# From which half batch on the feed-forward's input is turned by transposing DMAs: the 4th in place of the 6th

## The chip, the cores and the metric

The kernel runs on one core of one Trainium2 chip. The metric is the device time of one execution in microseconds (us). The engines of the core are named as the profile names them: PE (TensorE, matmuls), PEld (its weight loads), DVE (VectorE), ACT (ScalarE), POOL (GpSimd) and SP (SyncE, which here only issues DMAs). The core has 16 DMA engines.

## What is computed

Attention over 8 batches with 8 heads of 64 columns and 576 rows, with a mask that lets each block of 64 rows see itself and the blocks before it; then a feed-forward layer whose mixing step is a Fourier transform.

```python
scores = where(mask, q @ k.T / 8, -1e9)
attn   = softmax(scores) @ v                       # 64 heads of 576 x 64
x      = heads side by side                        # 8 batches, 576 x 512
u      = x + real(fft(fft(x, axis=1), axis=2))
un     = (u - mean(u)) / sqrt(var(u) + 1e-6)       # per row of 512
out    = u + relu(un @ w_ch1) @ w_ch2              # 512 -> 2048 -> 512
```

## The kernel before

All large matmuls run on halves of 16 bits: a number is split into a high part and a low part, and three products (high by high, high by low, low by high) replace one product of 32 bits.

**Stages.** For each head there are score matmuls (lines `scores`, out of the tiles `rest` and `lead`), a maximum over the scores (`max_part`, which reads `lead` alone), and value matmuls (`values`, into `av`). The rows of maxima are turned on PE (`shift`), shrunk on ACT to the small tile `mt` and copied by a DMA into one row of the head's `lead` tile, because the maximum is subtracted by the score matmul itself. Each batch of 8 heads then goes through the Fourier steps, and out of a batch come two half batches of 256 rows each (a lower and an upper one); the 64 rows that are left of each batch are gathered over four batches into one further half batch (the tiles `left`). So there are 18 half batches, numbered from 1: two for each of 8 batches, and the 9th and the 18th from the rows that are left. Each goes through normalization and through one feed-forward pass of matmuls (`first` into the tiles `h` and `ps`, `second` into `acc`).

**Heads and their tiles.** Heads are counted from 0. A head uses one of three pairs `lead0/rest0`, `lead1/rest1`, `lead2/rest2` in turn, so head 24 uses `lead0` and head 42 too. Queries and keys of two heads arrive together; their high and low parts are spread over the tiles by DMAs on SP's queue, `high_copies` (into `lead`, two DMAs of 64 x 576) and `low_copies` (into `rest`, two of 64 x 1152). The maximum of a head needs its high copies, its scores need the low copies and the `mt` copy as well.

**Turning.** The first feed-forward matmul needs the normalized rows `un` with the 512 columns on the partitions. There are two ways, and `BY_DMA` says from which half batch on the second is used:

```python
if me >= BY_DMA:      # norm, halve (ACT cast, DVE subtract), two transposing DMAs per 128 rows
    ...
    for n in range(2):
        sync.dma_start(parts[n][:, :, i], halves[:, n], transpose=True)
...
for c in range(NK):   # else four PE transposes of 128 x 128 per 128 rows, then ACT cast, DVE subtract
    tp(t[:, P * c:P * (c + 1)], un[:, P * c:P * (c + 1)], ident)
```

In the profile the PE transposes are the only instructions of L249; the copies of the second way are DMA_TRANSPOSE on SP's queue, `uh<-un` and `ul<-un`.

**The rows that are left.** For the second batch of each pair, after the last part of its Fourier step (matmuls of `zpc` and `zps`), four small DMAs gather 33, 31, 33 and 31 rows of 512 numbers into `left`:

```python
for at in (0, 64):
    sync.dma_start(mine[0][at:at + 33], X2[at:at + 33])
    sync.dma_start(mine[0][at + 33:at + 64], U2[at + 1:at + 32])
```

**Order.** The program is written by a planner at build time. Each piece of work is a `Step` with a cost on PE and a chain of costs on the other engines and on SP's queue (Q, M and L in a chain are the queue, the transfer and its latency); the planner keeps a clock of its own and issues the step that it takes to be ready, feed-forward matmuls as filler between the heads' work. Every engine runs its instructions in the order in which they were written, SP's queue too. A step that is added or taken away moves the planner's clock, and so the order of everything behind it. SP's DMAs carry one of eight counters in turn, so a DMA waits for the one eight places ahead of it.

Of the kernel before, what the change touches and what calls it, by code (L numbers as in the profile page):

```python
# [48 lines left out]
PSHIFT = 5  # L49


BY_DMA = 6
BANKS = {"ps": 3, "h": 2, "acc": 2}

ONCE = 17
# [164 lines left out]
def tile_attn_fourier_ffn(  # L220
# [857 lines left out]
    def normalized_steps(us, keys, stores, place):  # L1078
# [6 lines left out]
        def norm(i):  # L1085
# [11 lines left out]
            yield  # L1097
            if me >= BY_DMA and i == 0:
                yield from halve(i)

        def halve(i):
            un = uns.pop(i)
            halves = rows[i] = work.tile([P, 2, DM], F16, name="un", bufs=2)
            scalar.copy(halves[:, 0], un)
            yield
            vector.tensor_tensor(halves[:, 1], un, halves[:, 0], op=ALU.subtract)
            yield
# [27 lines left out]

        if me >= BY_DMA:
            free = (("F", me - 2),)
# [591 lines left out]
```

## Time and profile before

| | us |
|---|---|
| median of 3 timed runs (1200.2 to 1202.14) | 1201.1 |
| the profiled execution's own time | 1194.43 |
| its span, first to last instruction | 1192.6 |
| PE busy in it | 1116.1 (94%) |
| DVE, ACT, POOL busy | 744.6, 629.0, 479.6 |

The profiled execution is 6.7 us shorter than the median of the timed runs. Its span is read in three parts. Up to about 310 us PE is busy for 248.5 us and waits often; from 310 to 900 us heads and feed-forward passes run side by side and PE is nearly always busy; from 900 us on PE does feed-forward passes alone. The mean granted clock of PE is 0.987 of full speed. SP's queue holds 26 pairs of transposing DMAs, two for each of the half batches 6 to 18, the first at 454.3 us; the 40 PE transposes of half batches 1 to 5 end at 418.6 us.

### The profile page before, as it was taken

Reading aid. Unit: us, or ns where it says so; the run is one execution under the profiler, and the core shown is the slowest. Engines: PE = TensorE matmul, PEld = TensorE weight load, DVE = VectorE, ACT = ScalarE, POOL = GpSimd, SP = SyncE. Lnnn points to the kernel's source line nnn. Section 1 sums busy time; section 2 is a strip of 40 time slices with the busy share of each in tenths; the row PEclk is TensorE's granted clock in tenths of the full one; section 3 lists DMA queues with packets and bytes.
Section 4 is the critical chain, followed back from the end, with each engine's and each line's share of the span. In section 5 each row is a group of like instructions: output and inputs, shape, how many; then the busy total and the mean of one; then the engine's idle time right before and its main releaser. Section 6 shows DMA issues by size and latency. Waiting matters only on the chain.

```text
span 1192.6 us, 26123 instructions
## 1 busy us (share of the span) xinstructions
PE 1116.1 (94%) x10182; PEld 820.3 (69%) x10182; DVE 744.6 (62%) x1607; ACT 629.0 (53%) x1383; POOL 479.6 (40%) x621
## 2 busy tenths in 40 slices
PE   5766788999899999999999999999999999999998
PEld 4543465676677777777677777677766766888875
DVE  6886787677867767756476576666656434454421
ACT  5666768756775667656457557655223212334320
POOL 4452525444653535345224335443334210555410
PEclk9998989999899999999999999999999999999999
DMA  8776254343453238233335532460121021111100
GB/s 263 234 232 216 89 145 101 100 112 99 109 150 95 68 92 195 78 90 97 100 97 134 120 99 80 100 149 18 32 45 50 27 56 30 33 31 28 27 19 18
DMA packets 94049, 115.07 MB, mean 96 GB/s; under 512 B 37591, under 2 KB 64129, under 8 KB 93926
## 3 DMA queue, kind: packets, MB, share of 16 engines
q1 hardware_dynamic: 86582, 89.06, 28.2%
q10 hardware_dynamic: 4384, 16.78, 4.2%
q0 software_dynamic: 2960, 7.58, 2.3%
q8 instruction: 80, 1.31, 0.5%
q14 instruction: 43, 0.35, 0.1%
HBM read 58.50 MB, written 18.89 MB: 65 GB/s over the span
## 4 chain that ended last, share of the span: by engine, by line
PE 80%; DMA 5%; DVE 5%; POOL 3%; ACT 3%; issue 2%; SPq 0%; DVEq 0%; ACTq 0%; POOLq 0%
PE acc L246 28%; PE ps L246 26%; PE h L246 19%; PE av L246 7%; DMA lead<-mt 3%; POOL pl L213 2%; DVE W L213 1%; DMA lead<-rest 1%; POOL u L213 1%; DVE M L213 1%; ACT p L213 1%; ACT ph L213 1%; POOL ag L213 1%; DMA fs<-add 0%; SPq L213 0%
## 5 line engine op out<-in xcount | busy, mean ns | idle before, releaser
L213 POOL TENSOR_TENSOR pl<-p,ph 128x288 f16<-128x288 f32 (+1 forms) x256 | 262.8, 1037 | 352.3 <-ACT ph L213 183.1
L246 PEld LDWEIGHTS <-W 128*128 128x128 f16 x3456 | 331.0, 98 | 66.2 <-DVE M L213 6.3
L246 PE MATMUL acc<-W,gh 128*128 128x512 f16 (+1 forms) x1008 | 288.8, 369 | 0.0
L246 PE MATMUL ps<-uh,W 128*128 128x256 f16 x1184 | 217.0, 273 | 1.0 <-DVE M L213 1.0
L246 PE MATMUL h<-uh,W 128*128 128x256 f16 x1120 | 211.5, 275 | 4.9 <-DVE M L213 4.9
L246 PE MATMUL acc<-W,gl 128*128 128x512 f16 (+1 forms) x504 | 185.8, 369 | 1.0 <-DVE gl L213 1.0
L246 PE MATMUL ps<-ul,W 128*128 128x256 f16 x592 | 161.3, 272 | 0.0
L246 PE MATMUL h<-ul,W 128*128 128x256 f16 x560 | 153.7, 274 | 0.0
L246 PEld LDWEIGHTS <-ph 128*128 128x128 f16 x2112 | 132.2, 103 | 27.1 <-issue 3.9
L246 PEld LDWEIGHTS <-gh 128*128 128x128 f16 x1056 | 98.9, 99 | 69.5 <-issue 1.7
L213 DVE TENSOR_REDUCE M<-ps 128x1 fp32r<-128x320 f32 (+4 forms) x219 | 97.6, 480 | 66.4 <-PE ps L246 65.9
L246 PE MATMUL ps<-lead 73*128 73x288 f16 (+11 forms) x513 | 117.3, 293 | 13.6 <-ACT lead L213 6.2
L246 PE MATMUL av<-VH,pl 128*128 128x65 f16 (+1 forms) x963 | 116.7, 201 | 9.1 <-POOL pl L213 7.5
L246 PE MATMUL av<-VH,ph 128*128 128x65 f16 (+1 forms) x966 | 118.0, 203 | 1.9 <-ACT p L213 0.7
L246 PE MATMUL av<-VL,ph 128*128 128x64 f16 x960 | 116.3, 200 | 0.0
L246 PEld LDWEIGHTS <-pl 128*128 128x128 f16 x1056 | 103.1, 102 | 12.8 <-POOL pl L213 9.9
L213 ACT ACTIVATE p<-ps 128x288 f32<-128x288 f32 (+1 forms) x166 | 82.5, 498 | 46.3 <-PE ps L246 38.5
L213 ACT CAST ph<-p 128x512 f16<-128x512 f32 (+1 forms) x188 | 98.3, 523 | 4.9
L213 ACT ACTIVATE gh<-ps 128x512 f16<-128x512 f32 x74 | 44.0, 594 | 107.4 <-PE ps L246 105.9
L213 DVE SCALAR_TENSOR_TENSOR gl<-ps,gh 128x512 f16<-128x512 f32 x74 | 50.9, 688 | 79.4 <-ACT gh L213 78.7
L246 PEld LDWEIGHTS <-lead 73*128 73x128 f16 (+1 forms) x744 | 65.1, 103 | 40.5 <-issue 9.2
L246 PEld LDWEIGHTS <-gl 128*128 128x128 f16 x528 | 51.4, 97 | 57.1 <-DVE gl L213 2.7
(285 smaller groups left out, 1938.7 us busy)
## 6 DMA issues: line engine op xcount, KB each, us to landing
raw<-in_qk_dram SPq DMA_DIRECT2D x30, 576.0 KB
W<-in_moe_w_ch_dram ACTq DMA_DIRECT2D x14, 1024.0 KB
V<-in_v_dram SPq DMA_DIRECT2D x32, 320.0 KB
rest<-lead SPq DMA_DIRECT2D x64, 144.0 KB
rest<-rest SPq DMA_DIRECT2D x60, 144.0 KB
out_dram<-u SPq DMA_DIRECT2D x32, 256.0 KB
xd<-x SPq DMA_DIRECT2D x30, 256.0 KB
lead<-lead SPq DMA_DIRECT2D x60, 72.0 KB
```

Source lines behind the costliest of these rows:

```text
L213: x = f(*args, **kw)
L246: return tc.keep_in_program_order(nc.tensor.matmul(*args, **kw))
```

## The change

One number: half batches 4 and 5 (the upper half of the second batch, the lower half of the third) are turned by DMA too.

```diff
-BY_DMA = 6
+BY_DMA = 4
```

For these two half batches it takes away 16 PE transposes of 128 x 128, the 4 ACT casts and the 4 DVE subtractions that read their result out of PSUM; it adds 4 ACT casts and 4 DVE subtractions on `un` itself and 8 transposing DMAs on SP's queue. The program is the same up to the normalization of the 4th half batch, and the planner writes everything behind it in another order. Three places of that order follow.

**PE, at the 4th half batch.** The names: `lead_288` is `lead0` with head 24's high copies, `ps_4529` and `h_4559` take the transposes, `ph`, `pl` and `av` are values of head 22, `M_99` the maxima of head 23. Before, the two groups of transposes stand ahead of value matmuls, and head 24's maximum comes after 30 of these:

```order
L246 MATMUL ps_4455<-uh,W 128x256
L249 MATMUL ps_4529<-ident,un 128x128 x4
L246 MATMUL ps_4540<-ident,M_99 5x128
L246 LDWEIGHTS gh
L246 MATMUL acc<-W,gh 128x512
L246 LDWEIGHTS gh
L246 MATMUL acc<-W,gh 128x512
L246 LDWEIGHTS gl
L246 MATMUL acc<-W,gl 128x512
L249 MATMUL h_4559<-ident,un 128x128 x4
L246 LDWEIGHTS ph_4473
L246 MATMUL av<-VH_107,ph_4473 128x65
```

Now:

```order
L246 MATMUL h_4455<-ul,W 128x256
L246 LDWEIGHTS W
L246 MATMUL h_4455<-uh,W 128x256
L246 LDWEIGHTS lead_288
L246 MATMUL ps_4534<-lead_288 128x64
L246 LDWEIGHTS lead_288
L246 MATMUL ps_4534<-lead_288 128x64
L246 LDWEIGHTS lead_288
L246 MATMUL ps_4534<-lead_288 128x192
L246 LDWEIGHTS ph_4450
L246 MATMUL av<-VH_107,ph_4450 128x65
```

Behind the same 24 feed-forward matmuls, the same score matmuls of head 22 and the same turned maxima, head 24's maximum is now next: the 8 transposes are gone, and 3 matmuls into `acc` and 30 into `av` that stood ahead of it stand behind it.

**SP's queue at the same place.** `X_120` and `U_121` are the Fourier rows that are left; `lead_288<-lead_288` and `lead_288<-rest_289` are head 24's high copies. Before:

```order
L213 DMA left<-X_120 33x512 [waits DMAHW7_49,Pool_49]
L213 DMA left<-U_121 31x512 [waits DMAHW0_49,DMASW7_49,Pool_49]
L213 DMA left<-X_120 33x512 [waits DMAHW1_49]
L213 DMA left<-U_121 31x512 [waits DMAHW2_49,DMASW4_49]
L213 DMA lead_288<-lead_288 64x576 [waits DMAHW3_49,PE_49,Activation_49]
L213 DMA lead_288<-rest_289 64x576 [waits DMAHW4_49,Activation_49]
L213 DMA xd<-x 128x4x128 [waits DMAHW5_49,DVE_49]
L213 DMA xd<-x 64x128 [waits DMAHW6_49]
L213 DMA V<-in_v_dram 128x640 [waits DMAHW7_49,DVE_49]
L213 DMA lead_245<-mt 1x5x128 [waits DMAHW0_49,Activation_49]
L213 DMA rest_289<-rest_289 64x1152 [waits DMAHW1_49,DVE_49]
L213 DMA rest_289<-lead_288 64x1152 [waits DMAHW2_49,DVE_49]
```

Now, from the second of the copies on:

```order
L213 DMA lead_288<-rest_289 64x576 [waits DMAHW4_49,Activation_49]
L213 DMA xd<-x 128x4x128 [waits DMAHW5_49,DVE_49]
L213 DMA xd<-x 64x128 [waits DMAHW6_49]
L213 DMA lead_245<-mt 1x5x128 [waits DMAHW7_49,Activation_49]
L213 DMA V<-in_v_dram 128x640 [waits DMAHW0_49,DVE_49]
L213 DMA_TRANSPOSE uh<-un 128x4x128 [waits DMAHW1_49]
L213 DMA_TRANSPOSE ul<-un 128x4x128 [waits DMAHW2_49,DVE_49]
L213 DMA rest_289<-rest_289 64x1152 [waits DMAHW3_49,DVE_49]
```

Up to the second `xd<-x` the queue is unchanged, head 24's high copies behind the four copies of left rows included; the first pair of new transposes stands ahead of the low copies of heads 24 and 25 and of head 25's high copies.

**SP's queue at the next rows that are left** (fourth batch). Before, the `mt` copy of head 43 follows them after two `xd` copies:

```order
L213 DMA left<-U_121 31x512 [waits DMAHW1_49,DMASW6_49]
L213 DMA xd<-x 128x4x128 [waits DMAHW2_49,DVE_49]
L213 DMA xd<-x 64x128 [waits DMAHW3_49]
L213 DMA lead_535<-mt 1x5x128 [waits DMAHW4_49,Activation_49]
```

Now the `mt` copy of head 42 follows, with two low copies and a load of 576 KB between:

```order
L213 DMA left<-U_121 31x512 [waits DMAHW4_49,DMASW6_49]
L213 DMA xd<-ZT 2x256 [waits DMAHW5_49]
L213 DMA rest_536<-rest_536 64x1152 [waits DMAHW6_49]
L213 DMA rest_536<-lead_535 64x1152 [waits DMAHW7_49]
L213 DMA raw<-in_qk_dram 128x1152 [waits DMAHW0_49]
L213 DMA lead_288<-mt 1x5x128 [waits DMAHW1_49,Activation_49]
```

Another head's `mt` copy is the first behind the left rows, and more stands between.

## The prediction

> **What bounds the kernel now.** I read the page's shares first, then the stretches, then who makes PE wait.
>
> ```profile
> PE 1116.1 (94%) x10182; PEld 820.3 (69%) x10182; DVE 744.6 (62%) x1607; ACT 629.0 (53%) x1383; POOL 479.6 (40%) x621
> PE 80%; DMA 5%; DVE 5%; POOL 3%; ACT 3%; issue 2%; SPq 0%; DVEq 0%; ACTq 0%; POOLq 0%
> ```
>
> PE is 94% busy and 80% of the chain that ended last. The stretches of time say where the rest is:
>
> ```profile
> 0.00:310.00 310.00, 248.47 (x2169) 174.22 (x2170) 235.06 (x501) 207.86 (x471) 141.47 (x171) 0.95 0.53 157
> 310.00:600.00 290.00, 282.32 (x2932) 207.85 (x2929) 196.62 (x457) 180.03 (x401) 129.35 (x151) 1.00 0.41 107
> 600.00:900.00 300.00, 298.71 (x2842) 215.75 (x2841) 190.71 (x432) 159.46 (x348) 121.22 (x140) 1.00 0.34 87
> ```
>
> (Columns: length; busy time of PE, PEld, DVE, ACT, POOL; granted clock, DMA share, GB/s.) The program is unchanged up to the 4th half batch's normalization, near 317 us. Behind it PE is idle for 290 - 282.32 = 7.7 us up to 600 us and for 1.3 us up to 900 us. So there the end is set by PE work plus PE's few waits, and these waits are, from 310 us to the end:
>
> ```profile
> PE ps L246 <- DMA lead<-rest: 2.9, 2, 1.6
> PE h L246 <- DMA lead<-mt: 2.8, 1, 2.8
> PE h L246 <- DMA lead<-rest: 2.0, 1, 2.0
> PE ps L246 <- DVE M L213: 1.0, 1, 1.0
> PE acc L246 <- DVE gl L213: 1.0, 2, 0.7
> ```
>
> Most of the 9.7 us are waits for head copies. Whatever moves PE's arrival against such a copy moves the end.
>
> **The change part by part: the transposes.** The timeline of PE at the 5th half batch prices a group of four (the other group stands right ahead of it):
>
> ```profile
> 418.12 0.60 PE L249 MATMUL ps<-ident,un 128*128 128x128 f32 x4
> 418.56 0.27 PE L246 MATMUL ps<-uh,W 128*128 128x256 f16 x1
> ```
>
> From start to start a group costs 0.44 us, so the four groups that go are 1.76 us of PE. More is not there to gain from PE work. What replaces them, by tile `un`:
>
> ```profile
> L213 ACT CAST un<-un x26: 602/617/620, 421.7 to 1110.0; 128x512 f16<-128x512 f32 x26
> L213 DVE TENSOR_TENSOR un<-un x26: 680/691/1284, 422.4 to 1110.7; 128x512 f16<-128x512 f32 x26
> L213 SPq DMA_TRANSPOSE uh<-un x26: 1190/1225/2513, 454.3 to 1112.5; - x26
> ```
>
> Casts and subtractions read PSUM before and SBUF now, four of each both times; ACT and DVE are 62% and 68% busy from 310 to 600 us (180 and 197 of 290), so a few hundredths there are hidden behind PE: 0. The eight DMAs hold SP's queue for 8 x 1.22 = 9.8 us. What stands behind a pair comes up to 2.5 us later: the low copies of heads 24 and 25 and head 25's high copies at the first place, of which the nearest user, head 25's maximum, stands some 11 us of PE work behind head 24's in the new order. I put 0, and up to 2.5 us if the cover is gone.
>
> **The first place: the copies of head 24.** PE at the 4th half batch:
>
> ```profile
> 317.19 0.27 PE L246 MATMUL ps<-uh,W 128*128 128x256 f16 x1
> 322.62 0.39 PE L246 MATMUL acc<-W,gl 128*128 128x512 f16 x1 [0.31 <-DVE gl L213]
> 322.84 0.60 PE L249 MATMUL h<-ident,un 128*128 128x128 f32 x4
> 323.28 0.19 PE L246 MATMUL av<-VH,ph 128*128 128x65 f16 x1
> 324.15 0.19 PE L246 MATMUL av<-VH,pl 128*128 128x65 f16 x1
> 326.36 0.30 PE L246 MATMUL h<-lead 72*128 72x64 f16 x3 [2.02 <-DMA lead<-rest]
> 326.82 0.60 PE L246 MATMUL acc<-W,gh 128*128 128x512 f16 x2
> 327.48 0.59 PE L246 MATMUL acc<-W,gh 128*128 128x512 f16 x2
> ```
>
> From 317.19 (where the orders part) to 324.34 PE works through the rows shown ahead, then it waits 2.02 us for head 24's high copies. In the new order the same stretch lacks 8 transposes (0.88 us), 3 matmuls into `acc` (327.48 - 326.82 = 0.66) and 30 into `av` (323.28 to 324.15, 0.9), and the 0.31 us wait for `gl` goes with the `acc` group. So PE stands before head 24's maximum at 324.34 - 0.88 - 0.66 - 0.9 - 0.31 = 321.6. When do the copies land? SP's queue:
>
> ```profile
> 317.50 0.64 SPq L213 DMA_DIRECT2D left<-U  x1
> 318.18 0.80 SPq L213 DMA_DIRECT2D left<-X  x1
> 319.08 0.63 SPq L213 DMA_DIRECT2D left<-U  x1
> 319.81 0.52 SPq L213 DMA_DIRECT2D lead<-lead  x1
> 320.42 0.55 SPq L213 DMA_DIRECT2D lead<-rest  x1
> ```
>
> They are issued back to back with the left rows, nothing on SP waits for data, and yet they land near 326.2, 5.8 us after their issue. The left rows are the reason I see. Where they run alone (late in the program) the DMA share is one engine's sixteenth:
>
> ```profile
> 1058.00:1059.00 1.00, 1.00 (x12) 0.90 (x10) 1.00 (x2) 0.00 (x0) 0.96 (x3) 1.00 0.07 27
> ```
>
> At 27 GB/s the two copies of 31 rows, 62 x 2 KB = 127 KB, take 4.7 us on that engine, from about 319 on, and the copies' shares on it stand behind. [...] SP's queue is unchanged up to these copies, so they land at the same time, and PE now waits from 321.6 to 326.36: 4.8 us in place of 2.33. When it goes on, it still has the 30 and the 3 matmuls to do: 0.9 + 0.66 = 1.6 us behind. The 0.88 us of transposes taken away here gained nothing, since they lay ahead of a wait that ends when the DMA does. Those of the 5th half batch (417.7 to 418.6 us) lie where PE never stands still, so their 0.88 us is gained:
>
> ```profile
> 400.00:450.00 50.00, 50.00 (x523) 35.62 (x522) 35.69 (x87) 32.63 (x75) 25.77 (x34) 1.00 0.36 94
> ```
>
> Net idle and work: 1.6 - 0.9 = +0.7 us. Bounds: copies that land before 321.6 make it -1.76 - 2.33 = -4.1; copies a microsecond later make it +1.7.
>
> **What a wait of 4.8 us does to the clock.** Stretches of 3.41 us ahead of the half-clock spans, and three that were followed by none:
>
> ```profile
> 107.09:110.50 3.41, 1.23 (x3) 0.47 (x3) 2.02 (x6) 3.35 (x9) 0.81 (x2) 1.00 0.59 125
> 110.50:120.75 10.25, 6.94 (x21) 4.63 (x21) 5.99 (x13) 4.15 (x10) 0.44 (x3) 0.50 0.48 163
> 294.83:298.24 3.41, 1.53 (x7) 0.51 (x7) 3.24 (x14) 1.40 (x3) 2.64 (x4) 1.00 0.61 213
> 298.24:308.48 10.24, 7.54 (x68) 5.17 (x67) 8.58 (x14) 8.66 (x21) 7.53 (x10) 0.50 0.30 70
> 189.01:192.42 3.41, 1.60 (x10) 0.82 (x10) 3.36 (x11) 3.41 (x7) 0.00 (x0) 1.00 0.00 0
> 322.13:325.54 3.41, 1.91 (x36) 1.53 (x35) 3.25 (x5) 3.41 (x10) 2.29 (x2) 1.00 0.72 216
> 564.48:567.89 3.41, 1.89 (x23) 1.04 (x21) 1.14 (x3) 2.61 (x5) 2.83 (x4) 1.00 0.20 60
> ```
>
> A stretch with PE busy for 1.23 or 1.53 of 3.41 us was followed by 10.24 us at half clock; one with 1.60, 1.91 or 1.89 was not. The spans begin on one grid (298.24 - 110.50 = 55 x 3.413), and 322.13 lies on it. A wait of 4.8 us leaves at most 1.0 us of work in one of two neighbouring stretches, wherever the grid lies. So the half clock comes, and of its 10.24 us some 9.4 us are PE work at half speed: +4.7 us. That PE makes this up later is unlikely, since hardly a wait follows (9.7 us in the whole list, 2.3 of them here). [...] The rows show the half clock after stretches that were not idle, so I take 4.7.
>
> **The second place: the next left rows.** SP and PE there:
>
> ```profile
> 561.56 0.62 SPq L213 DMA_DIRECT2D left<-U  x1
> 563.43 0.73 SPq L213 DMA_DIRECT2D lead<-mt  x1
> 569.13 0.28 PE L246 MATMUL h<-lead 73*128 73x288 f16 x1 [2.76 <-DMA lead<-mt]
> ```
>
> The same pattern holds an `mt` copy for over 5 us and costs 2.76 us. In the new order head 42 is hit; its `mt` copy has a load and two low copies more ahead of it (a sixteenth of 576 KB and 2 x 144 KB is 54 KB, at 27 GB/s an estimated 2 us on the slow engine), and PE does some 1.4 us more work between, counted in the order. I take +0.6 us; from -2.76 (PE comes later than the copy) to +2, and a further 4.7 us if the clock falls there too.
>
> **Sum.** -0.9 + 1.6 + 4.7 + 0.6 = +6.0 us on the profiled execution's own 1194.43 us (its span 1192.6 and 1.8 around it): 1200.4. The timed median is 1201.1, 6.7 us above that execution. Its 2.0 and 2.8 us waits would put too little work into a stretch for some positions of the grid, so I suppose that timed runs pay the half clock at these places part of the time, and carry over +4 of the 6: 1201.1 + 4 = **1205 us**.
>
> **The rivals.** (1) No change: the timed runs before already pay the half clock at the first place, or it does not come. Then -0.9 + 1.6 + 0.6 = +1.3: 1202.4. [...] For the first: the unexplained 6.7 us. Against both: 1.91 us of work in the stretch at 322 us and no half clock, and half clock behind stretches with 1.23 and 1.53 us of work. (2) Faster: head 24's copies no longer hang on the left rows. `V`, 320 KB, is issued one place later than before; if it is that load which delays them, they land earlier, each microsecond earlier is one gained, and below 324.8 us the change pays: at 321.6 it is -4.1 and no extra half clock, 1197.0. Against it: the two copies of 31 rows stand ahead of them either way. (3) Slower still: the second place also falls to half clock and a transposing pair ahead of an `mt` copy opens a wait of up to 2.5 us: 6.0 + 4.7 + 2.5 - 2 = +11, 1212. Half clock there is decided by whether the wait passes about 3 us. Against it: 26 pairs stand in SP's queue before, and the list of waits above is short.
>
> **How the numbers follow.** Forecast 0.48, rival 1 0.22, rival 2 (with any other lucky order) 0.15, rival 3 0.15. A measurement of this kernel tells a change from none at about 0.2%, 2.4 us. Slower by more: 0.48 + 0.15 = 0.63; within: 0.22; faster: 0.15. The range from 1197.5 to 1212 reaches from rival 2 to rival 3 and leaves out about 0.15; the forecast's own range is 1203.5 to 1208.
>
> **What would show it.** In the changed profile: 24 PE transposes in place of 40 and 30 transposing DMAs into each of `uh` and `ul`; a PE wait of some 4.8 us for `lead<-rest` at 321 to 327 us and a granted clock of 0.50 for 10 us behind it; a wait for `lead<-mt` of 3 us or more at the fourth batch's left rows. I am wrong if PE does not wait over 3 us at the first place, or if the clock stays at 1.00 behind it; and a gain of more than 4 us would mean that waits I have not counted went away in the new order.

## The result

The changed kernel takes 1206.99 us (median of 10 runs, 1205.43 to 1212.83) beside 1200.65 us of the kernel before on the same chip (10 runs, 1197.15 to 1206.38). The ratio is 1.0061, with a 95% interval of 1.0046 to 1.0077: 6.3 us slower. Timed a second time (the ninth experiment) the ratio was 1.0085 (1.0059 to 1.0111).

The profiled execution of the changed kernel took 1206.64 us, its span 1204.8. The page answers the two rows shown of before so:

```profile
PE 1118.8 (93%) x10166; PEld 820.3 (68%) x10166; DVE 744.3 (62%) x1607; ACT 627.9 (52%) x1383; POOL 473.7 (39%) x621
PE 79%; DMA 6%; DVE 6%; POOL 3%; ACT 3%; issue 2%; SPq 1%; DVEq 0%; ACTq 0%; POOLq 0%
```

PE has 16 instructions fewer (10166 for 10182), and they are not shorter in sum: 1118.8 us busy against 1116.1, since more of them ran at half clock (mean granted clock 0.967 against 0.987). By stretches (same columns as before):

```profile
310.00:600.00 290.00, 280.65 (x2839) 204.91 (x2837) 190.76 (x450) 176.17 (x392) 124.26 (x148) 0.99 0.43 109
600.00:900.00 300.00, 294.10 (x2857) 212.56 (x2856) 178.62 (x413) 157.19 (x349) 112.54 (x133) 0.99 0.34 87
```

PE now stands idle for 9.4 us in the first stretch (7.7 before) and for 5.9 in the second (1.3 before). The list of waits from 310 us on:

```profile
PE ps L246 <- DMA lead<-rest: 7.4, 3, 4.7
PE ps L246 <- DMA lead<-mt: 3.6, 1, 3.6
PE h L246 <- DMA lead<-mt: 3.2, 1, 3.2
PE acc L246 <- DVE gl L213: 0.7, 1, 0.7
PE h L246 <- DMA rest<-lead: 0.4, 1, 0.4
```

These are 15.3 us where the five rows before were 9.7, and four waits make 13.8 of them. **The first place** is the one forecast:

```profile
323.70 0.27 PE L246 MATMUL h<-uh,W 128*128 128x256 f16 x1
328.69 0.33 PE L246 MATMUL ps<-lead 72*128 72x64 f16 x3 [4.72 <-DMA lead<-rest]
```

**The second** (3.2 us, at 577.8 us) is head 42's `mt` copy behind the fourth batch's left rows. **The third** (3.6 us, at 668.5 us) was not on my list. ACT writes head 49's `mt` rows:

```profile
663.41 0.27 ACT L213 ACTIVATE mt<-ps 5x128 f16<-5x128 f32 x1 [0.59 <-PE ps L246]
```

and SP, which has to send them, is still busy with a transposing pair and with the loads of the next batch's rows:

```profile
662.74 1.28 SPq L213 DMA_TRANSPOSE uh<-un  x1
664.11 1.22 SPq L213 DMA_TRANSPOSE ul<-un  x1
665.39 1.36 SPq L213 DMA_DIRECT2D X<-xd  x2
666.79 0.41 SPq L213 DMA_DIRECT2D u<-xd  x1
667.30 0.77 SPq L213 DMA_DIRECT2D lead<-mt  x1
```

The rows are ready at 663.7, leave at 667.3, and PE goes on at 672.13. The kernel before has a pair there too (654.4 to 656.9 us); the `mt` rows behind it were ready at 658.0 us and left at 659.3, and PE did not wait for them. The fourth wait is 2.3 us for `lead<-rest`, from 792.0 to 794.3 us; before, 1.3 us were waited there.

**The clock.** Three of the four waits were followed by half clock. In pairs, the stretch of 3.41 us with the wait and the next one:

```profile
325.42:328.83 3.41, 0.14 (x4) 0.17 (x5) 0.14 (x1) 2.58 (x7) 2.80 (x4) 1.00 0.76 180
328.83:332.24 3.41, 3.41 (x25) 1.87 (x23) 2.65 (x6) 0.00 (x0) 0.00 (x0) 0.50 0.74 95
578.00:581.41 3.41, 0.41 (x4) 0.33 (x4) 1.36 (x4) 0.04 (x1) 0.79 (x2) 1.00 0.19 70
581.41:584.83 3.42, 3.42 (x26) 1.93 (x25) 0.91 (x3) 3.15 (x7) 1.46 (x2) 0.50 0.00 0
670.16:673.57 3.41, 1.44 (x13) 1.08 (x13) 0.00 (x0) 1.03 (x3) 0.05 (x1) 1.00 0.38 136
673.57:676.98 3.41, 3.41 (x15) 1.67 (x14) 0.56 (x2) 2.84 (x7) 2.33 (x3) 0.50 0.00 0
```

Each time it lasted one stretch of 3.41 us, in which PE was busy throughout. In the second of them a 128x512 matmul takes 0.43 us from start to start (582.16 to 582.59 us) and 0.22 us behind it (585.42 to 585.64), so each cost 1.7 us, half of the stretch.

**The account.** From the first left rows on SP (316.12 us before, 318.66 after) to the issue of the last group of stores (1187.46 and 1199.61) it is 871.3 us before and 881.0 after: +9.6. Waits + (15.3 - 9.7) = 5.6, half clock 3 x 1.7 = 5.1, transposes -1.76: +8.9. Three waits of 0.2 us each, which the changed kernel's list has below the five rows shown and the list of before has not, make up most of the rest. The other 2.5 us of the difference between the two profiled executions lie ahead of the first left rows, in work that is the same in both.

### The profile page after: what moved, and what is told of

The parts are those of the page before. It is cut to its first block, busy times and chain, and to the rows that moved or that the text cites. A ratio compares the mean times of both kernels' runs of the same rounds, so it can differ in the third digit from the quotient of the medians.

```text
span 1204.8 us, 26104 instructions
## 1 busy us (share of the span) xinstructions
PE 1118.8 (93%) x10166; PEld 820.3 (68%) x10166; DVE 744.3 (62%) x1607; ACT 627.9 (52%) x1383; POOL 473.7 (39%) x621
## 4 chain that ended last, share of the span: by engine, by line
PE 79%; DMA 6%; DVE 6%; POOL 3%; ACT 3%; issue 2%; SPq 1%; DVEq 0%; ACTq 0%; POOLq 0%
PE acc L246 27%; PE ps L246 26%; PE h L246 18%; PE av L246 7%; DMA lead<-mt 3%; DVE W L213 2%; POOL pl L213 2%; DMA lead<-rest 1%; DVE M L213 1%; POOL u L213 1%; SPq L213 1%; ACT p L213 1%; ACT ph L213 1%; DMA raw<-in_qk_dram 1%; DMA fs<-add 0%
## 5 line engine op out<-in xcount | busy, mean ns | idle before, releaser
L213 POOL TENSOR_TENSOR pl<-p,ph 128x288 f16<-128x288 f32 (+1 forms) x256 | 257.4, 1015 | 342.4 <-ACT ph L213 165.9
L213 DVE TENSOR_REDUCE M<-ps 128x1 fp32r<-128x512 f32 (+4 forms) x205 | 91.1, 478 | 59.6 <-PE ps L246 59.0
L213 ACT ACTIVATE p<-ps 128x512 f32<-128x512 f32 (+1 forms) x172 | 86.1, 502 | 67.6 <-PE ps L246 60.6
```

The lines of the kernel that those rows point to most:

```text
L213: x = f(*args, **kw)
```

## The experiments

Theory A: the new order brings PE to head copies that are held up in SP's queue and on the DMA engine that carries the 31-row copies, and each long wait is followed by half clock. Theory B: the transposing DMAs, or the new order as such, cost the time. The ratios are all to the kernel before, timed beside it on the same chip. "Stretch" is the time from the first left rows to the last group of stores, where the program ahead of it is the same.

| kernel | ratio (95%) | stretch, us |
|---|---|---|
| before, two profiles | 1 | 871.3, 871.6 |
| changed; again (9) | 1.0061 (1.0046 to 1.0077); 1.0085 (1.0059 to 1.0111) | 881.0; 883.8 |
| 1 changed, cut | 1.0011 (0.9990 to 1.0031) | 874.6 |
| 2 before, cut | 0.9935 (0.9920 to 0.9950) | 869.5 |
| 3 changed, waits filled | 0.9980 (0.9967 to 0.9993) | 877.5 |
| 4 from the 5th half batch | 1.0007 (0.9994 to 1.0021) | 877.3 |
| 6 changed, head 49's mt by ACT | 1.0019 (1.0003 to 1.0034) | 875.9 |
| 7 changed, cut, mt by ACT | 0.9949 (0.9928 to 0.9969) | |
| 8 before, cut, mt by ACT | 0.9935 (0.9912 to 0.9957) | |
| 10 changed, left rows by POOL | 1.0010 (0.9993 to 1.0027) | |
| 11 before, left rows by POOL | 1.0021 (1.0002 to 1.0041) | |
| 12 changed, cut, mt by ACT, left rows later | 0.9935 (0.9910 to 0.9961) | |

### 1 and 2: the 31-row copies cut, in both kernels

```diff
-    sync.dma_start(mine[0][at + 33:at + 64], U2[at + 1:at + 32])
+    sync.dma_start(mine[0][at + 33:at + 49], U2[at + 1:at + 17])
+    sync.dma_start(mine[0][at + 49:at + 64], U2[at + 17:at + 32])
```

> The changed kernel with each 31-row copy of left rows cut in two, 16 rows and 15 rows; the order of everything else is the changed kernel's. Theory A (the changed order meets head copies held up by the 31-row copies): head 24's copies are issued some 1.2 us later but no longer stand behind 4.7 us of left rows on one engine, so the first place's wait of 4.7 us falls to 1 to 2.5 us, the second place's 3.2 us to under 1 us, and no half clock follows either; with 1.7 us of half clock saved at each that is some 7 us: 1199 to 1201 us against 1207. The wait of 3.6 us for an mt copy near 668 us stays. Theory B (the time is lost to the transposing DMAs on SP's queue or to the new order as such, the left rows being innocent): both waits stay within 1 us of what they were, 1206 to 1208 us.

> The kernel before with the same cut of the 31-row copies. Theory A: its waits for head copies behind left rows (2.0 us at the first place, 2.8 us at the second) go, up to 4.8 us: 1196 to 1198 us. With both kernels cut, the change's own price is what is left: the 1.76 us of transposes gained, the 3.6 us wait with its half clock near 668 us lost, so the cut changed kernel stands 1 to 5 us above the cut kernel before. Theory B: the kernel before does not move, 1200 to 1202 us, and the gap between the two stays 6 us.

The changed kernel gained 0.5%, about 6 us, as Theory A has it. Its waits:

```profile
PE ps L246 <- DMA lead<-mt: 3.2, 1, 3.2
PE ps L246 <- ACT gh L213: 2.8, 1, 2.8
PE h L246 <- DMA lead<-mt: 2.7, 1, 2.7
PE ps L246 <- DMA lead<-rest: 2.6, 1, 2.6
```

The first place is the row with 2.8 (the page names ACT; the last packets of head 24's copies end 0.5 us before PE goes on, in the changed kernel 0.7 us before). The copies' last packets show the cause: uncut, the trace's packet records have the last 8 of 128 packets at 327.62 to 328.01 us, directly behind a row of 2 KB packets, one every 0.08 us as on one engine, that ends at 327.62; cut, the 128 end at 325.00. That is 4.5 us behind the end of the copy's issue uncut, and 1.2 us cut. So the 31-row copies did hold head 24's copies, for 3.3 us, of which the two more rows on SP took some back. No half clock follows here or at the second place (one span is left, behind the third). The second place missed its forecast: 2.7 us and not under 1. Its `mt` rows now take 2.2 us to land instead of 5.4, but leave SP later, since the queue got two more rows and the load ahead took 1.8 us:

```profile
570.06 1.83 SPq L213 DMA_DIRECT2D raw<-in_qk_dram  x1
571.99 0.78 SPq L213 DMA_DIRECT2D lead<-mt  x1
```

They were ready at 568.1, so the queue itself held them for 3.9 us.

The kernel before gained more than forecast, 0.65%, and beats both uncut kernels. Its wait at the first place is gone, and the 2.8 us at the second shrank to

```profile
PE h L246 <- DMA lead<-mt: 0.4, 1, 0.4
```

In it PE comes to head 24's copies later, so that the cut is enough; in the changed order it is not. At the fourth place its wait grew from 1.3 to 2.0 us (at 794.5 us), and a half clock follows that one (at 795.98 us), which the uncut kernel's two profiles do not have. The gap between the two cut kernels is 0.76%, 9 us where 1 to 5 were expected, while by the traces it is 5.1 us: the timed pair alone speaks for Theory B as much as for A.

### 3: the waits filled with work nobody reads

```diff
+    def fill(t, count):
+        for _ in range(count):
+            mm(t, W[:, 0, 0, 0:P], W[:, 1, 0], start=True, stop=True)
...
+        if h == 24 and n == 0:      # in max_part
+            fill(t, 16)
...
+        if n == 0 and h in (42, 49):    # in scores
+            fill(t, 8)
```

> The changed kernel with matmuls put into its three longest waits, whose results nobody reads (the next matmul into the same bank starts it anew): 16 of 128x512 ahead of head 24's maximum (3.5 us of the 4.7 us wait), 8 ahead of head 42's first scores (1.7 of 3.2 us) and 8 ahead of head 49's (1.7 of 3.6 us). Theory H (the half clock behind these waits costs 1.7 us each): the waits shrink by what the matmuls take, no stretch at 0.50 follows at 329, 581 and 674 us, and the time is 4 to 5 us lower: 1202 to 1203 us. Rival (the half clock is made up in later waits, or timed executions do not pay it): unchanged, 1206 to 1208 us.

```profile
321.00 3.61 PE L246 MATMUL ps<-W 128*128 128x512 f16 x16
325.55 0.30 PE L246 MATMUL ps<-lead 72*128 72x64 f16 x3 [0.94 <-DMA lead<-rest]
```

The matmuls took 3.61 us of the first wait and left 0.94, and the half clock behind the first and the second place is gone. Behind the third it stayed: the wait happened to be longer in this execution, and 2.9 us of it were left. The stretch is 877.5 us, 3.5 less than in the changed kernel's first profile, which is two half clocks of 1.7. So these two were paid for in full and not made up later. The timed gain is larger than forecast (0.8% with an uncertainty of some 0.2%, where 3.5 us are 0.3%); the trace does not show where the rest comes from.

### 4: one of the two half batches alone

```diff
-BY_DMA = 4
+BY_DMA = 5
```

> Turned by transposing DMAs from the 5th half batch on: the 4th keeps its PE transposes. Theory A: the first place is the kernel before's (wait 2 us, no half clock), head 43's mt copy and not head 42's stands behind the fourth batch's left rows, and 0.88 us of transposes are gained: 1199 to 1201 us. Theory B, transposing DMAs cost by themselves: half of the change's 6 us, 1203 to 1205 us. A third possibility: each order has waits of its own at other copies, and this one is anywhere from 1198 to 1207 us, to be read from its list of waits.

1.0007: within what can be told from no change. As timed, the 0.6% of the whole change is not the sum of two equal halves, which speaks against Theory B in its simple form; the trace does not say it as plainly, for its stretch is 6.0 us longer than before (3.4 us more idle time of PE, 1.7 of half clock, 0.9 not accounted for). The third possibility came true, since this order has its own waits (three for `lead<-mt`, 1.4 at most, 2.8 for `M`, 2.1 at the first place). At the first place it has the kernel before's order, and yet:

```profile
322.99:326.40 3.41, 1.35 (x35) 1.21 (x32) 2.37 (x4) 2.79 (x7) 1.42 (x2) 1.00 0.60 179
326.40:329.82 3.42, 3.38 (x11) 1.45 (x12) 2.08 (x5) 0.83 (x2) 0.00 (x0) 0.50 0.67 159
```

A wait of 2.1 us was enough for a half clock where the grid of 3.41 us lay so that 1.35 us of work were left in the stretch.

### 5 and 9: both kernels again

> The kernel before, unchanged, profiled a second time. Its first profiled execution took 1194.4 us, 6.7 below the timed median, while the changed kernel's agrees with its median. Theory C (timed executions of the kernel before pay a half clock behind its 2.0 us and 2.8 us waits, which the first profile did not show): a second profile shows a span of half clock near 324 or 568 us, and is 1 to 3 us longer from the first left rows (316 us) to the end. Rival (the spread is in the unchanged work up to 316 us): the first left rows come 3 us or more later than 316.1 us, the rest takes the 876 us that it took.

> The changed kernel, unchanged, timed again beside the kernel before and profiled a second time. Theory A: the same three waits (4.7, 3.2 and 3.6 us) and a half clock behind each, 881 us from the first left rows to the last store as in the first profile (871.3 and 871.6 in the two of the kernel before), and a ratio of 1.005 to 1.008. Rival (the order of events after 310 us differs between executions as much as the work before does): that stretch differs by 3 us or more from 881, with other waits.

The kernel before's second profile has its span at 1197.2 us, 4.6 longer, and the first left rows on SP at 320.43 us in place of 316.12. Behind them everything took as long as before (871.6 us). No half clock shows there; the stretch with the first place's wait, 2.2 us, kept 1.73 us of work:

```profile
326.68:330.10 3.42, 1.73 (x35) 1.52 (x35) 3.01 (x5) 3.42 (x9) 2.05 (x2) 1.00 0.75 219
```

So 4.3 of the 4.6 us are in the unchanged work ahead, and Theory C fell in these two profiles. The changed kernel's second profile repeats the three waits and lengthens the third and the fourth:

```profile
PE ps L246 <- DMA lead<-rest: 7.3, 2, 4.7
PE ps L246 <- DMA lead<-mt: 4.5, 1, 4.5
PE h L246 <- DMA lead<-mt: 3.2, 1, 3.2
```

The fourth, 2.6 us, now has a half clock behind it too (at 794.79 us). The stretch was 883.8, within 3 us of the first; the ratio, 1.0085, is just above the forecast 1.005 to 1.008. Both kernels thus have an order of events from 316 us on that repeats.

### 6: the third place alone

```diff
-    sync.dma_start(both(h)[0][KM:KS, 0:640]...
+    (scalar if h == 49 else sync).dma_start(both(h)[0][KM:KS, 0:640]...
```

> The changed kernel with one copy given to another queue: head 49's mt rows are sent off by ACT, which wrote them, and not by SP, where they stood behind a transposing pair and three loads from xd. Theory A: the copy leaves at 664 instead of 667.3 us, ahead of the loads, and lands before PE needs it at 668.5; the wait of 3.6 us and the half clock of 1.7 us behind it go: 5 us less, 1201 to 1203 us. Rival (that wait is made up by what follows, or another copy holds PE at the same place): within 1.5 us of the changed kernel, 1205.5 to 1208.5 us.

```profile
663.84 1.30 ACTq L213 DMA_DIRECT2D lead<-mt  x1
```

The rows leave on ACT's queue at 663.84 and not on SP's at 667.30. In the list of waits the third place is now

```profile
PE ps L246 <- DMA lead<-mt: 1.1, 1, 1.1
```

in place of 3.6 us; no half clock follows, the time falls by 0.42% (1.0061 to 1.0019), 5 us, as forecast. This one copy in SP's queue was the dearest of the places. The half clocks at the other two lasted two stretches here:

```profile
326.39:329.80 3.41, 2.48 (x22) 1.67 (x23) 1.48 (x4) 0.23 (x2) 0.57 (x1) 0.50 1.07 173
329.80:333.22 3.42, 3.42 (x9) 1.21 (x8) 2.78 (x6) 0.00 (x0) 0.00 (x0) 0.50 0.42 97
```

In the first half-clock stretch PE was busy for 2.48 us only, and it was followed by another; the next was full, and full clock came back.

### 7 and 8: all three places eased, in both kernels

Beside the cut of experiment 1:

```diff
-    sync.dma_start(both(h)[0][KM:KS, 0:640]...
+    scalar.dma_start(both(h)[0][KM:KS, 0:640]...
```

> The changed kernel with the 31-row copies cut in 16 and 15 and all mt rows sent off by ACT, so that all three places are eased. Theory A: the waits at the second and third place go (2.7 and 3.2 us with the cut alone), the first is at most 2.8, and no half clock follows from 310 us on: some 7 us below the cut changed kernel, 1194 to 1197 us, about 1 us from the kernel before treated alike. Theory B (the new order or the transposing DMAs cost by themselves): 3 us or more above the kernel before treated alike.

> The kernel before with the same two edits. Its waits for mt rows are small once the left rows are cut (0.4 us), so sending them off by ACT gains under 1 us and may cost ACT as much: 1193 to 1195 us. What counts is the gap to the changed kernel treated alike: Theory A from -1.8 us (its transposes) to +1; Theory B +3 us or more.

The changed kernel falls to 0.9949, the kernel before to 0.9935: the gap is 0.14% +- 0.3%, 1.7 us, just above what Theory A gave (up to 1 us) and below Theory B's 3; the uncertainty holds both. What the changed kernel still waits for more than the other is

```profile
PE ps L246 <- DMA lead<-rest: 3.1, 2, 2.9
PE ps L246 <- DMA lead<-mt: 1.6, 1, 1.6
```

with a half clock behind the 2.9 us at the first place, which the expectation had ruled out. There head 24's parts were written by 320.2 us, but their copies left SP at 326.4, behind the left rows, which had themselves waited for POOL.

### 10 to 12: the left rows out of the way

All with the cut and the `mt` rows sent by ACT. In 10 and 11 POOL, which adds up the left rows, also sends them:

```diff
-    sync.dma_start(mine[0][at:at + 33], X2[at:at + 33])
+    gpsimd.dma_start(mine[0][at:at + 33], X2[at:at + 33])
...    # the two cut copies likewise
```

In 12 they stay with SP, as a step of their own that becomes due when the additions are done:

```diff
+        def left_rows():
+            ...    # the six copies
...
             yield from second_stage(2)
+            yield Step(left_rows, 0.0, ("Q0.1",), (D_("u", 2),), D_("left"), place=place)
```

> The changed kernel with the left rows (31-row copies cut) sent off by POOL, which wrote them, in place of SP, and all mt rows by ACT. With the cut and ACT alone a wait of 2.9 us was left at the first place: head 24's high copies were ready at 320.2 us and stood on SP behind the left rows until 326.4. Theory A: now they leave at once, that wait and the half clock of 1.7 us behind it go, some 4 us below that version: 1188 to 1191 us beside a kernel before of 1200, ratio 0.990 to 0.993. Theory B (the new order or the transposing DMAs cost by themselves): no better than 0.994. POOL's own issues may cost: then a wait for POOL shows near 330 or 570 us.

> The kernel before with the same edits. It has no wait left at the first place with the cut and ACT, so left rows on POOL gain it nothing: 0.993 to 0.995. The gap between the two kernels treated alike is the change without its waits: Theory A -1.8 us (16 transposes) to 0, Theory B +2 us or more.

> The changed kernel with the 31-row copies cut, mt rows sent off by ACT, and the left rows made a step of their own behind the additions, so that SP sends head 24's high copies ahead of them instead of behind. POOL is spared (its issues of the left rows cost 3.3 us ahead of the normalization and put the time at 1.001). Theory A: no wait over 2 us is left for a copy at the first place and no half clock follows; against the same kernel with left rows ahead (0.995) that is 2.9 + 1.7 us less: 0.990 to 0.992, the best of all. Theory B: 0.994 or more. The step moves the planner's order behind 316 us once more, so a new wait at another copy, of up to 4 us, is possible; the list of waits would name it.

On POOL it failed as a gain: both kernels got some 0.6 to 0.9% slower than in 7 and 8. Head 24's copies left at 316.0 us, but PE still waited 2.4 us at the first place, now for ACT:

```profile
323.09 0.95 DVE L213 TENSOR_SCALAR un<-u,ag 128x512 f32<-128x512 f32 x1 [3.34 <-POOL ag L213]
...
324.08 0.62 ACT L213 CAST un<-un 128x512 f16<-128x512 f32 x1 [3.28 <-DVE un L213]
...
324.94 0.26 ACT L213 ACTIVATE mt<-ps 5x128 f16<-5x128 f32 x1
...
325.25 0.22 PE L246 MATMUL ps<-lead 72*128 72x64 f16 x2 [2.35 <-ACT mt L213]
```

POOL's six issues stand ahead of the normalization's `ag`, DVE waits 3.34 us for it, and ACT waits 3.28 us before the cast of `un` that the change put there, with the `mt` rows that empty PE's bank behind it (from 324.94 us on). A half clock follows this wait (at 326.85 us) and another a wait of 1.7 us for `lead<-rest` (at 784.24 us). As a comparison the pair is of use: treated alike the changed kernel is 0.11% below the other. In 12 SP sends head 24's copies first; the longest wait for any copy from 310 us on is

```profile
PE ps L246 <- DMA lead<-rest: 0.3, 1, 0.3
```

and no half clock follows one. The ratio, 0.9935, is short of the forecast 0.990 to 0.992: it equals that of experiment 8, and beats both kernels of this case (1189.13 us beside 1196.60). Since the step moves the planner's order once more, 12 and 8 are not a pair that differs in the change alone.

**What follows.** The traces let the gap between the changed kernel and the kernel before be put down term by term. From the first left rows to the end of PE's last matmul, in the kernel before and the changed kernel as they are (columns as in the stretches above):

```profile
316.12:1187.30 871.18, 861.52 (x7940) 640.65 (x7936) 502.96 (x1088) 417.55 (x905) 334.85 (x446) 1.00 0.29 75
318.66:1199.44 880.78, 865.09 (x7924) 641.95 (x7919) 502.37 (x1087) 416.42 (x905) 329.62 (x446) 0.99 0.30 75
```

The gap is 9.6 us. PE is idle for 15.7 us in place of 9.7, and the three stretches at half clock cost 5.1; take both off, and -1.5 us are left. The same for each pair treated alike, in us:

| pair | gap by trace | idle time of PE | half clock | left | gap as timed |
|---|---|---|---|---|---|
| as they are | +9.6 | +6.0 | +5.1 | -1.5 | +6.3 |
| as they are, again (5 and 9) | +12.2 | +7.3 | +6.8 | -1.9 | +10.2 |
| cut (2 and 1) | +5.1 | +6.7 | 0 | -1.6 | +9 |
| cut, mt by ACT (8 and 7) | +3.4 | +3.2 | +1.7 | -1.5 | +1.7 |
| and left rows by POOL (11 and 10) | -0.6 | -1.4 | +1.7 | -0.9 | -1.3 |

What is left is -0.9 to -1.9 us in all five pairs, close to the -1.76 us of the 16 transposes, so nothing remains that the transposing DMAs or the new order would cost beyond PE's idle time and its half clock. Nor do the eight transposing DMAs that the change adds stand ahead of a copy that PE waits long for: in the changed kernel SP issues them from 326.52 to 437.26 us, head 24's copies before them at 322.35 and 322.97, and the other three long waits come at 578 us and later. Theory A stands: the change's price is the waits that its order runs into, with their half clocks. As timed, the gap is +0.6 to +0.85% as they are, +0.76% with the cut alone, +0.14% with the cut and ACT and -0.11% with POOL; the last two are within their uncertainty of no difference, and a gain as small as the transposes' (0.15%) cannot be seen there. Why the cut pair's timed gap is 4 us above that of its traces stays open. Experiment 10 shows one exception, to B's credit: the cast that the change put on ACT ahead of the `mt` rows became a wait there, 2.35 us of PE, when its input was late.

## Why the prediction was right, point by point

The time, 1205 us with slower as the likeliest, came true at 1207, and the mechanism forecast, a longer wait for head 24's copies with half clock behind it, is there. That the number came so close is in part luck: the half clock at the first place was put 3 us too high, while a place worth 5 us and the half clock at the second place were missing from the sum.

1. **The transposes.** 16 are gone from PE, and 30 transposing DMAs stand in each of the two rows by tile:

```profile
L213 SPq DMA_TRANSPOSE uh<-un x30: 1189/1230/2252, 326.5 to 1124.6; - x30
```

The 0 for the copies behind the new pair at the first place was right: from 310 to 400 us PE waits for no copies but head 24's. The 0 for the moved cast held in the changed kernel, and fell in experiment 10, where its cover was gone.

2. **The first place.** 4.8 us forecast, 4.7 measured, in both profiles, and the cause named was the right one in part. Cutting the 31-row copies took away 1.9 of it and the half clock; in experiment 12, where the copies are sent ahead of the left rows, no wait over 0.3 us for any copy is left. So the copies were late for two reasons, the engine and the queue, and I had named the first. Rival 2 (`V` holds them) is out: `V` stood behind them and the wait was unchanged. That one engine carries a 31-row copy is read from its packets, one every 0.08 us; the traces do not name a packet's engine, and why it would be one for 31 rows no run shows. What experiment 1 shows is the price: with 16 and 15 rows the copies behind landed 1.2 us after their issue and not 4.5.

3. **The half clock: the term that was mis-sized.** It came, as the busy time in the stretch said, and lasted 3.41 us where I had taken 10.24: 1.7 us, not 4.7. My rows of 10.24 us were from places where PE stood idle on and off during the half clock too (6.94 and 7.54 us busy of 10.24), and the 9.4 us of work that I took for it come from no row. Behind 316 us, in all traces, it ended after a stretch in which PE was busy for 2.79 us or more, mostly throughout, and went on behind the two with 2.42 and 2.48 (experiment 6). What brings it on is about as I read it: 0.14, 0.41, 1.44 and 1.35 us of work were followed by it, 1.73 and 1.91 were not. But no amount of work divides the two cleanly. In experiment 10 a stretch with 1.66 us was followed by it (780.83 us), in experiment 11 one with 1.53 was not (894.09 us), and ahead of 316 us a fuller one was, in the changed kernel:

```profile
294.70:298.11 3.41, 2.12 (x28) 1.50 (x28) 1.64 (x6) 1.16 (x7) 2.87 (x5) 1.00 0.89 257
298.11:311.76 13.65, 10.01 (x76) 6.14 (x75) 11.67 (x25) 10.83 (x24) 9.42 (x14) 0.50 0.34 104
```

Its end is no cleaner: at the first and second place full clock came back behind one full stretch (3.41 and 3.42 us busy), but ahead of 316 us the half clock also outlasted one (3.40 us of work from 309.62 to 313.03 us in the second profile of before, and half clock up to 316.45). Had I priced one stretch of 3.41 us, the term would have been 1.7.

4. **The second place.** +0.6 forecast, +0.4 measured (3.2 for 2.8), and the half clock that I left to rival 3 came here as well: +1.7. Rival 3's bound of about 3 us holds at this place: waits of 2.7 and 2.8 us (experiments 1 and 5, and before) brought none, waits of 3.2 us did. It does not hold elsewhere, where 2.0 and 2.1 us were enough (experiments 2 and 4).

5. **What was missing.** The third place: 3.6 us and 1.7 of half clock, 5 us by experiment 6. Rival 3 had its kind ("a transposing pair ahead of an `mt` copy opens a wait of up to 2.5 us"), but with 0.15 and without a place. I had looked along the new order only where left rows stand. At the fourth place 1.0 us more was waited. Against these stand two waits of before, 1.6 us at 474 and 1.0 us at 528 us, that went away.

6. **The sum and the carrying over.** +6.0 was forecast from 316 us on, +9.6 and +12.2 (883.8 - 871.6) were measured: too small by the third place, above all. I then took 2 us off for timed runs in which the kernel before pays its own half clocks. The timed differences, 6.3 us and 0.85% (10.2 us), are 3.3 and 2.0 below those of the traces, so the size was about right; the reason given is not shown. Two profiles of before have no half clock behind 316 us, the order's twin in experiment 4 has one. In every row of the first table that has a stretch, the timed difference is some 2 to 9 us below that of the traces, so timed runs of the kernel before seem longer than its two profiles say. Where is left open: the spread of the work ahead of 316 us (4.3 us between two profiles of one program) hides it.

## What to carry to other kernels

When a change lets a planner put the work into another order, walk the whole new order for each copy that the bounding engine needs, and ask when its data are written, what stands ahead of it in its queue and what shares its engines; the places at which the old order waits are only some of those at which the new one can. Cut copies whose packets come one after the other, as those of the 31-row copies did (one every 0.08 us), and send small urgent rows from the engine that writes them: together these edits took 1.1% off the changed order (1.0061 to 0.9949), more than the choice between the orders. In the order of before the cut alone was worth its 0.65%, and sending the rows from ACT added nothing. Price a clock penalty by how soon the engine is fully busy again, not by the longest one in the profile: at the three places of the changed kernel's first profile the half clock lasted 3.41 us, and the rows that I priced it by last 10.24.

## What the runs showed of the hardware

The spans at half clock begin on a grid of 3.41 us: those of the changed kernel at 328.83, 581.41 and 673.57 us lie 74 and 27 times 3.413 us apart. Behind 316 us, in all the traces, half clock followed 17 times, each time a stretch in which PE was busy for 1.66 us or less; one such stretch, with 1.53 us (experiment 11), was not followed by it, and none with 1.68 or more was. So a wait of 1.7 us (experiment 10) can be enough and one of 2.8 us (before) not, by where the grid lies. Ahead of 316 us it also followed fuller stretches (2.12 us), so PE's busy time as the profile gives it does not alone decide. A full stretch of it cost 1.7 us (two of them 3.5 us in experiment 3), and filling a wait with matmuls nobody reads avoided it at two places there. A small copy of 5 rows took 5.4 us from the end of its issue until PE went on behind 31-row copies (575.6 to 581.0 us in the changed kernel), and 2.2 us behind the same rows cut (572.8 to 575.0 in experiment 1). Sending the six left-row copies took POOL 3.3 us (318.87 to 322.17 in experiment 10), in which its next work stood behind.
